# First four weight tiles turned on TensorE, first two tiles' matmuls by gradient quarters, column tables made behind the first rows

## Chip, cores and metric

One core of one Trainium2 chip runs the kernel. The metric is the device time of one execution in microseconds (us). TensorE (PE), VectorE (DVE), ScalarE (ACT) and GpSimd (POOL) compute; SyncE (SP) issues almost all DMAs. Each engine works through its own instructions in the order in which the program wrote them.

## The reference, cut to what matters

The forward pass of two blocks and all its gradients are computed in one launch, in bfloat16, with S = 2048, D = 448, F = 1792.

```python
def _A_ref(x, w_r, w_i):                    # spectral block
    X = rfft2(x.astype(float32)); X = X * (w_r + 1j * w_i)
    return irfft2(X, s=(S, D)).astype(bfloat16)

def _B_ref(x, w1, b1, w2, b2):              # MLP along the tokens
    h = _layernorm(x)
    u = gelu(einsum("bsd,sf->bdf", h, w1) + b1)
    return transpose(einsum("bdf,fs->bds", u, w2) + b2)

h  = x + _A_ref(_layernorm(x), A_w_r, A_w_i)
h2 = h + _B_ref(_layernorm(h), B_w1, B_b1, B_w2, B_b2)
# outputs: h2 and, from grad_out, the gradients of x, w_r, w_i, w1, b1, w2, b2
```

The part that the change touches first is one product of the backward pass, dg = w2 · grad_out (1792 x 2048 times 2048 x 448). It needs no result of the forward pass, only two inputs, so the kernel uses its matmuls as filling.

## The kernel before

**Stages.** First the forward Fourier transform: for each of 16 row groups, `row_a` (four 128-wide matmuls against a 128 x 128 table that is scaled by the layer norm, `scale_R`) and, three rows later, `row_b` (four 226-wide matmuls against the column tables `csF`). Each result is copied out of PSUM by `evac`, which picks ACT or DVE by a running estimate of their loads. After two rows of `row_b` a DMA on SP (line 668) reshapes the result into `D2`. Then `s2_stage` (line 671): four sets of small matmuls, the multiplication by the spectral weights on DVE (`w_mult`), small matmuls back, and 16 DMAs on SP (line 697) that reshape into `D3`. Then `inv_rows` (line 722), which needs all of `D3`, gives h. Then the MLP forward, backward and the spectral block backward. PE is nearly always busy behind `inv_rows`.

**The filling.** `dg_gen` (line 791) yields once per matmul of dg: 14 tiles of 128 rows of w2, each 16 matmuls of 448 columns that accumulate in one PSUM bank. `fill(n)` takes n of them at a place in the program. By the start of `s2_stage` 117 are taken, in the stage 95, the other 12 behind it. All 224 must be done before `inv_rows` is written.

**Its weights.** The matmul needs w2's tile with the tokens on the partitions, so `load_w2T` (line 301) loads it with a transposing DMA (line 306) on SP, into a ring of five buffers. Three are issued at the start, two in the row loop (`t in (1, 3)`), and then one whenever a tile is finished. Above `CAP` = 8 a finished tile's load is held back until the row loop is over (lines 907 to 909).

**Orders that matter.** SP's queue at the start is x rows 0 and 1, tile 0, x rows 2 and 3, four quarters of grad_out (`load_go`) among the rest of x, tiles 1 and 2, then the biases and the spectral weights (18 DMAs, line 573, spread over the row loop by `W_AT`). DVE and ACT make the 128-table (`gen_R`) and the column tables (`gen_fwd_d`: two chains on DVE, then two Sine activations on ACT) before the first layer norm statistics (`ln_stats`: line 82 is the helper that records every DVE and ACT instruction). ACT loads another function table when it goes from Sine to Sqrt and back; that is done at line 820 and at the first Sine of `gen_UV`. PE begins with 26 matmuls on zeros (line 360).

**Biases.** `load_biases` returns `turn`, called in `s2_stage` (line 914): two transposing DMAs on SP (line 786) and two copies on POOL that wait for them.

**PSUM.** `ps_mm()` gives one of four banks in turn, `ps_ff()` one of four others. Line 218 is every matmul but the small ones (line 223) and the transposes of `gen_inv_d` (line 545).

Of the kernel before, what the change touches and what calls it, by code (L numbers as in the profile page):

```python
# [10 lines left out]
BF16 = mybir.dt.bfloat16  # L11
# [6 lines left out]
P = 128  # L18
# [16 lines left out]
RESH_LAG = 1.1  # L35
ML_F = 4
SIDE = 2
CAP = 8
N_FILL_F = (6, 3, 20, 3, 24, 2)
N_FILL_B = (16, 16, 30, 8, 24, 8)  # L40
INV_SD = 1.0 / float(S * D)
# [81 lines left out]
def kernel(  # L123
# [54 lines left out]
    def ps_mm():  # L178
        return psum.tile([P, 512], F32, tag="mm", bufs=4, name="ps_mm")


    def evac(out, in_, scale=None):
        n = int(np.prod(in_.shape[1:]))
        if load[0] + sc.cost('copy', n, False) <= load[1] + ve.cost('tensor_copy', n, in_.dtype == BF16):
            if scale is None:
                sc.copy(out=out, in_=in_)
            else:
                sc.activation(out=out, in_=in_, func=ACT.Copy, scale=scale)
        elif scale is None:
            ve.tensor_copy(out=out, in_=in_)  # L190
        else:
            ve.tensor_scalar(out=out, in0=in_, scalar1=scale, scalar2=None, op0=ALU.mult)
# [24 lines left out]
    def mm(out, lhsT, rhs, start, stop):  # L217
        nc.tensor.matmul(out, lhsT=lhsT, rhs=rhs, start=start, stop=stop)  # L218
        clock[0] += int(np.prod(rhs.shape[1:])) / 2400.0
        run_due()  # L220
# [80 lines left out]
    def load_w2T():  # L301
        j = w2T_ring.i
        if j == NFB:
            return
        wT = w2T_ring.next()
        nc.sync.dma_start_transpose(out=wT, in_=B_w2[j * P:(j + 1) * P, :].rearrange("f (t c) -> f t c", c=P))  # L306
        w2Ts.append(wT)

    go_tp_d = grad_out[0].rearrange("(t p) d -> p t d", p=P)
    w2Ts = []  # L310

    def load_x(q):
        nc.sync.dma_start(out=xn[:, 4 * q:4 * q + 4, :], in_=x_pt[:, 4 * q:4 * q + 4, :])  # L313

    def load_go(q):
        nc.sync.dma_start(out=go_tp[:, 4 * q:4 * q + 4, :], in_=go_tp_d[:, 4 * q:4 * q + 4, :])  # L316
# [2 lines left out]
    load_w2T()  # L319
    nc.sync.dma_start(out=xn[:, 2:4, :], in_=x_pt[:, 2:4, :])  # L320
    load_go(0)
    load_go(1)
    load_x(1)
    load_go(2)
    load_go(3)
    load_x(2)
    load_x(3)
    load_w2T()
    load_w2T()
    gtail = rst[0:16, 2 * P:3 * P]  # L330
    gp_.memset(gtail, 0.0)
    nc.sync.dma_start(out=gtail[:, 0:64], in_=grad_out[0][S - 16:S, 3 * P:D])
# [24 lines left out]
    sc.activation(out=warm, in_=warm, func=ACT.Sin)  # L357
    nc.vector.memset(rAT[:, 0:512], 0.0)
    idle = ps_mm()
    for _ in range(26):  # L360
        nc.tensor.matmul(idle[:, 0:D], lhsT=rAT[:, 0:P], rhs=rAT[:, 0:D], start=True, stop=True)

    pcol = col()
# [55 lines left out]
    def gen_fwd_d():  # L419
        t = ftmp(576, 2, KW)  # L420
        t2 = ftmp(1028, 2, KW)
        q = ftmp(1536, 2, KW)
        q2 = ftmp(2048, 2, KW)
        js = []
        for o in (1.0, 225.0):
            js.append(col())
            ve.tensor_scalar(out=js[-1], in0=pcol, scalar1=2.0 / 896.0, scalar2=o / 896.0, op0=ALU.mult, op1=ALU.add)
        chains = []
        for w, u, v, ph in ((1, t, q, 0.0), (0, t2, q2, 0.25)):
            chain = []  # L430
            v_, s_ = Later(ve, chain), Later(sc, chain)
            for b in range(2):
                v_.tensor_scalar(out=u[:, b, :], in0=krow[:, 0:KW], scalar1=js[b], scalar2=ph, op0=ALU.mult, op1=ALU.add)
            v_.tensor_scalar(out=v, in0=u, scalar1=MAGIC, scalar2=MAGIC, op0=ALU.add, op1=ALU.subtract)
            v_.tensor_tensor(out=v, in0=u, in1=v, op=ALU.subtract)
            s_.activation(out=csF[:, w, :, :], in_=v, func=ACT.Sin, scale=s1)
            chains.append(chain)
        return [fn for pair in zip(*chains) for fn in pair]
# [159 lines left out]
    def scale_R(t):  # L598
        v = Rs_ring.next()
        ve.tensor_scalar(out=v, in0=Rm[:], scalar1=rstd_x[:, t:t + 1], scalar2=None, op0=ALU.mult)  # L600
        return v
# [33 lines left out]
    def row_a(t, R):  # L635
        pa = ps_ff()
        ft = folds[t // 2]
        for k in range(4):
            o = DC * (4 * (t % 2) + k)
            mm(pa[:, k * P:(k + 1) * P], lhsT=ft[:, o:o + P], rhs=R, start=True, stop=True)  # L640
        if t % 4 == 0:
            blks[t // 4] = blk_ring.next()
        evac(out=blks[t // 4][:, :, t % 4, :], in_=pa[:].rearrange("p (n x) -> p n x", x=8))
# [114 lines left out]
    def fill(n):  # L758
        while n > 0 and pending:
            try:  # L760
                next(pending[0])
                n -= 1
                if row_ops:
                    row_ops.pop(0)()
            except StopIteration:
                pending.pop(0)

    def drain():
        while pending:
            fill(1)  # L770
# [8 lines left out]
    def load_biases():  # L779
        gp_.memset(smr, 0.0)  # L780
        nc.sync.dma_start(out=smr[0:NFB, 0, :], in_=B_b1.rearrange("(j p) -> j p", p=P))
        nc.sync.dma_start(out=smr[:, 1, :], in_=B_b2.rearrange("(j p) -> j p", p=P))

        def turn():
            for i, dst in ((0, b1col), (1, b2col)):
                nc.sync.dma_start_transpose(out=smc[:, i, :], in_=smr[:, i, :])
                gp_.tensor_copy(out=dst[:], in_=smc[:, i, :])
        return turn


    def dg_gen():
        for j in range(NFB):
            wT = w2Ts.pop(0)
            pg = ps_mm()
            for t in range(NT):
                mm(pg[:, 0:D], lhsT=wT[:, t, :], rhs=go_tp[:, t, :], start=(t == 0), stop=(t == NT - 1))
                if t == NT - 1:
                    evac(out=dgu[:, j, :], in_=pg[:, 0:D])
                    if w2T_ring.i >= cap[0]:
                        held_w2.append(load_w2T)  # L800
                    else:
                        load_w2T()
                yield

    cap, held_w2 = [CAP], []
    pending.append(dg_gen())
# [4 lines left out]
    zero_pads()  # L811
    r_ops = []
    gen_R(Later(ve, r_ops), Later(sc, r_ops))
    fwd_ops = gen_fwd_d()
    for fn in r_ops:
        fn()
    for fn in fwd_ops:
        fn()
    nc.vector.memset(csF[:, 0, :, 0:1], 0.0)
    sc.activation(out=warm, in_=eps_x, func=ACT.Sqrt)  # L820
    base = ftmp(3072, 16, 16, 2)
    fix = ftmp(3584, 16)
# [9 lines left out]
        ln_stats(xn, t, mvx)  # L832
    sc.activation(out=rstd_x[:, 0:2], in_=mvx[:, 0:2, 1], func=ACT.Sqrt, bias=eps_x, scale=1.0)
    fold_prep(xn, 0)
    ve.tensor_scalar(out=ident[:], in0=krow[:, 0:P], scalar1=pcol, scalar2=None, op0=ALU.is_equal)
    ve.reciprocal(out=rstd_x[:, 0:2], in_=rstd_x[:, 0:2])
    Rs = {t: scale_R(t) for t in range(2)}
    for t in range(2, 4):
        ln_stats(xn, t, mvx)
    sc.activation(out=rstd_x[:, 2:4], in_=mvx[:, 2:4, 1], func=ACT.Sqrt, bias=eps_x, scale=1.0)  # L840
# [5 lines left out]
    gen_inv_cols(0)  # L846
    gen_inv_cols(1)
    fill(4)
    row_a(0, Rs.pop(0))
    for t in (4, 5):  # L850
        ln_stats(xn, t, mvx)
    for fn in rstd_of(4, 6):
        fn()
    fill(0)
    turn_biases = load_biases()
    Meter.side, Meter.every, Meter.count = [], 1, 0
    GROUPS = {0: (6, 8), 1: (8, 10), 3: (10, 12), 5: (12, 14), 7: (14, 16)}
    STATS = {0: (6, 7), 1: (8, 9), **{t: (t + 8,) for t in range(2, 8)}}
# [2 lines left out]
    for c in range(2):  # L861
        for e in range(2):
            sc.copy(out=Rp.rearrange("p (e a q b c) -> p c e a q b", e=2, c=2, q=8, a=2)[:, c, e],
                    in_=Rm[:, 64 * c + 32 * e:64 * c + 32 * e + 32].rearrange("p (q a b) -> p a q b", q=8, a=2))
    FILL_A = (4, 4, 4, 3, 3, 3, 3, 3, 3, 3, 3, 3, 3, 3, 3, 3)
    FILL_B = (0, 0, 0, 2, 2, 2, 2, 2, 2, 2, 2, 2, 2, 2, 2, 2)
    for t in range(NT):
        if t in (1, 3):
            load_w2T()
        if t + 1 < NT:  # L870
            row_a(t + 1, Rs.pop(t + 1))
        fill(FILL_A[t])
        if 1 <= t and t + 3 < NT:
            if t + 3 in (4, 8, 12):
                while Meter.side:
                    Meter.side.pop(0)()
            Rs[t + 3] = scale_R(t + 3)
        row_b(t - 3)
        if t == NT - 1:
            for i in range(t - 2, NT):  # L880
                row_b(i)
        if t % 2 and t < 12:
            fold_prep(xn, t // 2 + 2)
        for i in STATS.get(t, ()):
            ln_stats(xn, i, mvx)
        for _ in range(3 if t > 0 else 0):
            if next(uv, None):
                break
        if t in GROUPS:
            a, b = GROUPS[t]  # L890
            newton_gp(mvx[:, a:b, 1], rstd_x[:, a:b], slice(a, b))
        for _ in range(W_AT.get(t, 0)):
            next(w_loads, None)
        if t in INV_S:
            gen_inv_s(INV_S[t])
        if t == 2:
            gen_RT()
        fill(FILL_B[t])
# [8 lines left out]
    cap[0] = NFB  # L907
    while held_w2:
        held_w2.pop(0)()
    fill(30)  # L910

    def fwd_mult(s, j, x, y):
        if (s, j) == (2, 0):
            turn_biases()
        w_mult(x, set_of(W, s)[:, 2 * j:2 * j + 2], y, False)

    s2_stage(lambda s: set_of(Xs, s), fwd_mult, 9, 10, 0)
# [55 lines left out]
        nc.sync.dma_start(out=w2cs[i], in_=B_w2.rearrange("(j p) s -> p j s", p=P)[:, :, 256 * i:256 * i + 256])  # L973

    for i in range(3):
        load_w2c(i)
    inv_rows(h_consumer, N_FILL_F[5], Ring(aT_ring.views + [cut(rO, 1024, 4, P)]), (3, 7, 11, 15))
    norm_h(10)
# [2 lines left out]
    rstd_of_h(3)  # L981
    for t in range(12, NT):
        norm_h(t, t == 14)
    drain()
    nc.sync.dma_start(out=h_d.rearrange("(p t) d -> p t d", t=NT), in_=hn)

# [401 lines left out]
```

## Time and profile before

| | us |
|---|---|
| median of 3 runs | 355.53 (355.19 to 358.33) |
| the profiled execution, whole | 355.19 |
| its span in the profile | 353.4 |
| busy: PE, DVE, ACT, POOL | 333.7, 251.2, 196.9, 63.2 |

Rows of the timeline give start, duration, engine, line, operation, destination and source with their buffers, how many were merged, and in brackets how long the engine had been idle and what ended it. PE's matmul durations overlap, so its pace is read from start to start. "SPq" rows are SP's issues: the time is how long SP was taken by the instruction, not how long the transfer took. In the views by window each engine has busy time and number of instructions; then come the granted clock of PE (1.00 is full), the mean busy share of the 16 DMA engines (it can pass 1) and GB/s.

### The profile page before, as it was taken

The numbers are of one execution on the slowest core, as the hardware profiler recorded it, in microseconds if no ns is written. First come the engines' busy times: TensorE is split into PE (matmuls) and PEld (weight loads), VectorE is DVE, ScalarE is ACT, GpSimd is POOL, SyncE is SP. The second block draws the span as 40 slices with busy tenths as digits, with TensorE's granted clock in tenths as the row PEclk, the third lists the DMA queues.
The fourth block names the chain that finished last, engine by engine and source line by source line (L and its number), as shares of the span: only waits on it lengthen the run. The fifth ranks groups of instructions, "written<-read, shape, count | busy, mean of one in ns | idle before, by whom it ended". The sixth has DMA issues, their size and how long they took to land.

```text
span 353.4 us, 7799 instructions
## 1 busy us (share of the span) xinstructions
PE 333.7 (94%) x2819; PEld 174.1 (49%) x2819; DVE 251.2 (71%) x667; ACT 196.9 (56%) x430; POOL 63.2 (18%) x219
## 2 busy tenths in 40 slices
PE   8579989984999999999999999999999999999995
PEld 3346645442654555555555555554334434455552
DVE  8996426860594788858323888877489886589994
ACT  5458534543796653532331345557568877588872
POOL 5776000010132000001000211110000000055760
PEclk9989999998799999999999999999999999999999
DMA  8999999937985999679686789765889798998985
GB/s 213 302 180 180 180 255 196 195 109 211 314 229 225 299 355 249 168 189 297 168 192 159 170 186 184 182 99 167 234 237 243 242 252 238 282 248 262 228 309 203
DMA packets 147247, 78.03 MB, mean 221 GB/s; under 512 B 95688, under 2 KB 139976, under 8 KB 147080
## 3 DMA queue, kind: packets, MB, share of 16 engines
q1 hardware_dynamic: 146920, 77.13, 86.1%
q8 instruction: 22, 0.36, 0.4%
q10 hardware_dynamic: 288, 0.39, 0.3%
q14 instruction: 17, 0.14, 0.1%
HBM read 25.71 MB, written 22.04 MB: 135 GB/s over the span
## 4 chain that ended last, share of the span: by engine, by line
PE 82%; DMA 6%; DVE 4%; SPq 3%; ACT 2%; issue 1%; POOL 0%; DVEq 0%; ACTq 0%
PE ps_mm L218 66%; PE ps_ff L218 13%; DMA rE<-in_B_w_dram 3%; PE ps_ff L223 3%; DVE rS L82 2%; DMA r<-r 2%; DMA rO<-in_B_w_dram 1%; DVE r L82 1%; SPq L306 1%; SPq L573 1%; SPq L316 1%; SPq L668 1%; ACT rX L82 1%; SPq L313 0%; DVE rA L82 0%
## 5 line engine op out<-in xcount | busy, mean ns | idle before, releaser
L218 PEld LDWEIGHTS <-r 128*128 128x128 bf16 (+2 forms) x600 | 56.6, 107 | 50.7 <-issue 9.1
L218 PEld LDWEIGHTS <-rS 128*128 128x128 bf16 (+2 forms) x496 | 40.7, 98 | 36.6 <-issue 7.3
L82 ACT CAST rO<-ps_mm 128x512 bf16<-128x512 f32 (+1 forms) x70 | 37.3, 583 | 15.9 <-PE ps_mm L218 14.5
L218 PE MATMUL ps_mm<-rD,r 128*128 128x448 bf16 x224 | 44.5, 352 | 0.0
L218 PEld LDWEIGHTS <-rst 128*128 128x128 bf16 (+1 forms) x320 | 23.5, 97 | 31.3 <-issue 14.1
L218 PE MATMUL ps_mm<-rC,rE 128*128 128x448 bf16 x144 | 32.5, 360 | 4.1 <-DMA rE<-in_B_w_dram 2.3
L218 PE MATMUL ps_mm<-rB,r 128*128 128x448 bf16 x160 | 31.2, 352 | 0.1
L82 ACT CAST r<-ps_ff 128x452 bf16<-128x452 f32 x41 | 22.7, 587 | 11.5 <-PE ps_ff L223 6.2
L218 PE MATMUL ps_mm<-rG,rst 128*128 128x512 bf16 (+1 forms) x128 | 28.5, 380 | 0.3 <-ACT rO L82 0.3
L218 PE MATMUL ps_mm<-r,rst 128*128 128x512 bf16 (+2 forms) x144 | 27.4, 345 | 0.0
L82 ACT ACTIVATE r<-ps_mm,rstd_h 128x448 bf16<-128x448 f32 x16 | 10.1, 633 | 26.8 <-PE ps_mm L218 26.8
L82 DVE SCALAR_TENSOR_TENSOR r<-ps_mm,b2col,r 128x448 bf16<-128x448 f32 x16 | 10.9, 682 | 19.9 <-PE ps_mm L218 17.0
L82 ACT ACTIVATE r<-rC 128x448 bf16<-128x448 bf16 x16 | 9.1, 572 | 26.7 <-DMA out_dram<-r 20.5
L82 ACT ACTIVATE rG<-rG 128x896 bf16<-128x896 bf16 x14 | 13.3, 950 | 15.0 <-DVE rG L82 14.7
L218 PE MATMUL ps_mm<-rE,rS 128*128 128x448 bf16 x112 | 21.5, 352 | 0.0
L218 PEld LDWEIGHTS <-rO 128*128 128x128 bf16 (+1 forms) x165 | 15.1, 98 | 12.9 <-DMA rO<-in_B_w_dram 0.9
L82 ACT CAST rS<-ps_ff 128x512 bf16<-128x512 f32 x31 | 17.9, 580 | 5.7 <-PE ps_ff L218 5.3
L218 PEld LDWEIGHTS <-rE 128*128 128x128 bf16 x144 | 13.5, 99 | 14.2 <-DMA rE<-in_B_w_dram 2.5
L218 PE MATMUL ps_ff<-csI,rAT 113*128 113x224 bf16 (+1 forms) x108 | 20.3, 313 | 0.0
L1136 POOL TENSOR_SCALAR lcol<-lcol 128x1 f32<-128x1 f32 x16 | 8.5, 529 | 64.7 <-ACT r L82 64.7
L82 ACT CAST rAT<-ps_ff 113x512 bf16<-113x512 f32 x24 | 13.8, 584 | 10.6 <-PE ps_ff L218 10.3
L82 DVE SCALAR_TENSOR_TENSOR rA<-ps_ff,rA 128x448 bf16<-128x448 f32 x16 | 9.9, 619 | 12.0 <-PE ps_ff L218 11.9
(189 smaller groups left out, 602.6 us busy)
## 6 DMA issues: line engine op xcount, KB each, us to landing
out_dram<-rO SPq DMA_DIRECT2D x34, 256.0 KB
r<-in_B_w_dram SPq DMA_DIRECT2D x5, 1024.0 KB
r<-r SPq DMA_DIRECT2D x32, 113.0 KB
rS<-in_B_w_dram SPq DMA_DIRECT2D x4, 896.0 KB
r<-r SPq DMA_DIRECT2D x12, 226.0 KB
out_dram<-rG SPq DMA_DIRECT2D x10, 256.0 KB
rO<-in_B_w_dram SPq DMA_DIRECT2D x2, 1024.0 KB
rC<-in_grad_out_dram SPq DMA_DIRECT2D x4, 448.0 KB
```

What stands on the lines that cost most here:

```text
L82: fn(**kw)
L218: nc.tensor.matmul(out, lhsT=lhsT, rhs=rhs, start=start, stop=stop)
L223: nc.tensor.matmul(out, lhsT=lhsT, rhs=rhs, start=start, stop=stop)
L306: nc.sync.dma_start_transpose(out=wT, in_=B_w2[j * P:(j + 1) * P, :].rearrange("f (t c) -> f t c", c=P))
L316: nc.sync.dma_start(out=go_tp[:, 4 * q:4 * q + 4, :], in_=go_tp_d[:, 4 * q:4 * q + 4, :])
L573: nc.sync.dma_start(out=d_ap if store else sb, in_=sb if store else d_ap)
L668: defer(RESH_LAG, lambda: resh[0].dma_start(out=D2[u:u + 125:4, 8 * e:8 * e + 8].rearrange("p g c k -> p (g c k)"), in_=cs.rearrange("p x ...
L1136: gp_.tensor_scalar(out=m1, in0=ms, scalar1=-1.0 / D, scalar2=None, op0=ALU.mult)
```

## The change

Weight tiles 0 to 3 are loaded by plain DMAs into `rB` as they lie in memory. `turn_w2` transposes a tile by 16 PE transposes into two PSUM banks and copies each bank to the old place with one ACT copy of 1024 columns. Tile 0 is turned ahead of the first `row_a`, tile 1 behind the first four matmuls of dg, tiles 2 and 3 later. The first two tiles' matmuls are taken by quarters of grad_out: four of tile 0, four of tile 1, and so on. `gen_fwd_d` moves behind the first `row_a`, the identity matrix ahead. The plan of fills has the same sum up to `s2_stage` (117), with more in the rows t = 2, 3, 4 and 16 fewer behind the loop. `CAP` is 9, the idle matmuls are 20. The biases' transposing DMAs move to the weight loads behind `s2_stage`, and their copies to DVE behind `inv_rows`.

```diff
-CAP = 8
+CAP = 9
+N_NAT = 4
...
         wT = w2T_ring.next()
+        w2Ts[j] = wT
+        if j < N_NAT:
+            nc.sync.dma_start(out=w2n[:, j, :, :], in_=B_w2[j * P:(j + 1) * P, :].rearrange("f (t c) -> f t c", c=P))
+            return
         nc.sync.dma_start_transpose(out=wT, in_=B_w2[j * P:(j + 1) * P, :].rearrange("f (t c) -> f t c", c=P))
-        w2Ts.append(wT)
+
+    def turn_w2(j):
+        for h in range(0, NT, 8):
+            pt = ps_mm()[:].bitcast(BF16).rearrange("p (t c) -> p t c", c=P)
+            for t in range(8):
+                nc.tensor.transpose(pt[:, t, :], w2n[:, j, h + t, :], ident[:])
+            sc.copy(out=w2Ts[j][:, h:h + 8, :], in_=pt)
...
+    w2n = cut(rB, 0, N_NAT, NT, P)
...
     load_w2T()
     nc.sync.dma_start(out=xn[:, 2:4, :], in_=x_pt[:, 2:4, :])
     load_go(0)
+    load_w2T()
+    load_x(1)
     load_go(1)
-    load_x(1)
     load_go(2)
     load_go(3)
+    load_w2T()
     load_x(2)
+    load_w2T()
     load_x(3)
-    load_w2T()
-    load_w2T()
...
-    for _ in range(26):
+    for _ in range(20):
...
     def dg_gen():
-        for j in range(NFB):
-            wT = w2Ts.pop(0)
-            pg = ps_mm()
-            for t in range(NT):
...
+        pgs = {}
+        turns = {(0, 3): 1, (1, 15): 2, (2, 8): 3}
+        order = [(j, 4 * q + i) for q in range(4) for j in range(2) for i in range(4)]
+        for j, t in order + [(j, t) for j in range(2, NFB) for t in range(NT)]:
+            if not t:
+                pgs[j] = ps_mm()
+            mm(pgs[j][:, 0:D], lhsT=w2Ts[j][:, t, :], rhs=go_tp[:, t, :], start=(t == 0), stop=(t == NT - 1))
+            if (j, t) in turns:
+                turn_w2(turns[j, t])
...
-    fwd_ops = gen_fwd_d()
     for fn in r_ops:
         fn()
-    for fn in fwd_ops:
-        fn()
-    nc.vector.memset(csF[:, 0, :, 0:1], 0.0)
+    ve.tensor_scalar(out=ident[:], in0=krow[:, 0:P], scalar1=pcol, scalar2=None, op0=ALU.is_equal)
     sc.activation(out=warm, in_=eps_x, func=ACT.Sqrt)
...
-    ve.tensor_scalar(out=ident[:], in0=krow[:, 0:P], scalar1=pcol, scalar2=None, op0=ALU.is_equal)
     ve.reciprocal(out=rstd_x[:, 0:2], in_=rstd_x[:, 0:2])
     Rs = {t: scale_R(t) for t in range(2)}
+    turn_w2(0)
+    row_a(0, Rs.pop(0))
...
     fill(4)
-    row_a(0, Rs.pop(0))
+    fwd_ops = gen_fwd_d()
+    for fn in fwd_ops:
+        fn()
+    nc.vector.memset(csF[:, 0, :, 0:1], 0.0)
...
-    FILL_A = (4, 4, 4, 3, 3, 3, 3, 3, 3, 3, 3, 3, 3, 3, 3, 3)
+    FILL_A = (4, 4, 8, 12, 6, 3, 3, 3, 3, 3, 3, 3, 3, 3, 3, 3)
...
-        if t in (1, 3):
+        if t == 0:
             load_w2T()
...
-    fill(30)
+    fill(14)
...
-        if (s, j) == (2, 0):
-            turn_biases()
...
     for i in range(3):
+        if i == 2:
+            turn_biases()
         load_w2c(i)
...
+    place_biases()
     drain()
```

More of the change, by code (lines that the diff above doesn't have):

```diff
@@ L305, in load_w2T @@
         wT = w2T_ring.next()
+        w2Ts[j] = wT
+        if j < N_NAT:
+            nc.sync.dma_start(out=w2n[:, j, :, :], in_=B_w2[j * P:(j + 1) * P, :].rearrange("f (t c) -> f t c", c=P))
+            return
         nc.sync.dma_start_transpose(out=wT, in_=B_w2[j * P:(j + 1) * P, :].rearrange("f (t c) -> f t c", c=P))
-        w2Ts.append(wT)
+    def turn_w2(j):
[4 more added lines that the diff above has]
+            sc.copy(out=w2Ts[j][:, h:h + 8, :], in_=pt)
     go_tp_d = grad_out[0].rearrange("(t p) d -> p t d", p=P)
-    w2Ts = []
+    w2Ts = {}
+    w2n = cut(rB, 0, N_NAT, NT, P)
     def load_x(q):
@@ L786, in turn, with place @@
                 nc.sync.dma_start_transpose(out=smc[:, i, :], in_=smr[:, i, :])
-                gp_.tensor_copy(out=dst[:], in_=smc[:, i, :])
-        return turn
+        def place():
+            for i, dst in ((0, b1col), (1, b2col)):
+                ve.tensor_copy(out=dst[:], in_=smc[:, i, :])
+        return turn, place
     def dg_gen():
-        for j in range(NFB):
-            wT = w2Ts.pop(0)
-            pg = ps_mm()
-            for t in range(NT):
[L796 to L803, printed above, removed]
+        pgs = {}
[7 more added lines that the diff above has]
+                turn_w2(turns[j, t])
+            if t == NT - 1:
+                evac(out=dgu[:, j, :], in_=pgs.pop(j)[:, 0:D])
+                if w2T_ring.i >= cap[0]:
+                    held_w2.append(load_w2T)
+                else:
+                    load_w2T()
+            yield
     cap, held_w2 = [CAP], []
@@ L854 @@
     fill(0)
-    turn_biases = load_biases()
+    turn_biases, place_biases = load_biases()
     Meter.side, Meter.every, Meter.count = [], 1, 0
```

## The prediction

> **What bounds the kernel now.** The page's busy shares come first: PE is busy for 333.7 of 353.4 us, so time comes only from PE's holes or from work put on it. The view by windows says where the holes are.
>
> ```profile
> core 0: us, PE busy (x) PEld busy (x) DVE busy (x) ACT busy (x) POOL busy (x), PEclk, DMA share, GB/s
> 10.00:20.00 10.00, 4.27 (x31) 2.19 (x29) 9.06 (x38) 4.08 (x12) 7.57 (x34) 1.00 1.17 270
> 20.00:24.00 4.00, 4.00 (x21) 2.46 (x20) 3.85 (x14) 2.69 (x4) 2.86 (x14) 0.57 0.62 144
> 50.00:60.00 10.00, 8.40 (x131) 4.32 (x130) 4.82 (x10) 3.34 (x8) 0.00 (x0) 1.00 1.00 225
> 80.00:90.00 10.00, 5.04 (x29) 2.94 (x28) 0.27 (x1) 3.72 (x7) 0.00 (x0) 0.76 0.85 227
> ```
>
> Three holes: 5.7 us in 10 to 20, 1.6 in 50 to 60, 5.0 in 80 to 90. After the first and the third the granted clock falls to about a half. In 10 to 20 DVE is busy 9.06 of 10: it has no room. PE's timeline names what ended each hole, and the chain of waits does so for the third:
>
> ```profile
> 10.74 0.92 PE L218 MATMUL ps_mm<-rC,rE 128*128 128x448 bf16 x4 [0.54 <-DMA rC<-in_grad_out_dram]
> 13.05 0.92 PE L218 MATMUL ps_mm<-rC,rE 128*128 128x448 bf16 x4 [1.17 <-DMA rC<-in_grad_out_dram]
> 16.83 0.64 PE L218 MATMUL ps_ff<-rX,rS 128*128 128x128 bf16 x4 [1.58 <-DVE rS L82]
> 19.76 0.74 PE L218 MATMUL ps_mm<-rC,rE 128*128 128x448 bf16 x3 [2.29 <-DMA rE<-in_B_w_dram]
> ...
> 53.04 0.62 PE L223 MATMUL ps_ff<-r,Vt 32*32 32x452 bf16 x16 [1.38 <-DMA r<-rX]
> ...
> 56.37 1.69 PE L218 MATMUL ps_mm<-rC,rO 128*128 128x448 bf16 x8 [0.22 <-DMA rO<-in_B_w_dram]
> ```
>
> ```profile
> 79.14 0.99 ACT r L82 x2
> ...
> 81.86 5.39 DMA r<-r
> 87.25 0.35 issue
> 87.59 4.55 PE ps_ff L218 x23
> ```
>
> The row at 16.83 is `row_a(4)`: it waits for DVE, not for a load. The wait at 87.59 is for the last reshape into `D3`. Why that is late is in SP's queue:
>
> ```profile
> 8.25 10.87 SPq L306 DMA_TRANSPOSE rE<-in_B_w_dram  x2
> ...
> 51.91 4.25 SPq L306 DMA_TRANSPOSE rO<-in_B_w_dram  x2
> 56.26 9.14 SPq L306 DMA_TRANSPOSE rE<-in_B_w_dram  x3
> 65.50 1.99 SPq L306 DMA_TRANSPOSE rO<-in_B_w_dram  x1
> 67.59 3.28 SPq L697 DMA_DIRECT2D r<-r  x4
> 70.93 2.41 SPq L786 DMA_TRANSPOSE smc<-rst  x2
> 73.45 9.01 SPq L697 DMA_DIRECT2D r<-r  x12
> ```
>
> A transposing DMA holds SP for about 2 to 5 us, a plain load for about 0.5. From 51.91 to 82.46 SP has no pause: six transposes, then the 16 reshapes with two bias transposes between. The reshapes run behind their data and bunch at the end.
>
> **The front, step by step.** The idle matmuls end at about 7.7 instead of 8.8 (the last ones go at 0.18 each, six fewer). Transposes: those of line 545 took 0.27 for four (44.19 to 44.46 start to start), so 16 take 1.1 and all 64 take 4.3 us of PE. Bounds: 3.5 by the pace of 128-wide matmuls (0.22 for four), 6.9 by the length of the record (0.43 for four).
>
> The Trainium skill, TensorE: Matmul & The Clock Gate, part 4 (PE-mode transpose), speaks against this: about 275 ns for one transpose in a kernel, and transposes do not hold the clock up as matmuls do. By it 64 would be an estimated 17.6 us and the total some 13 us worse; the row at 44.19, at granted clock 1.00, says 0.07 us.
>
> The copies: eight of 1024 columns, all on ACT. A cast of 512 took 0.58, two in a row 1.07 (at 11.45): I take 0.97 each, between 0.95 (the 896-wide ACT row) and 1.16 (twice 0.58). What is queued behind them decides. ACT's order is: copies of tile 0, `row_a(0)`'s evacuation, the Sqrt for rows 2 and 3, copies of tile 1, Sine table, column tables. Tile 0's first half is turned at 8.4, so its copies end at 10.4, the evacuation (0.5) at 10.9, the Sqrt (0.3) at 11.2. DVE's reciprocal, at 10.76 before, waits for that Sqrt, and behind it stand in DVE's order: two scalings (0.5, to 11.7), the column chains now moved here (1.07 + 0.69 + 1.16 and two small ones, 3.1 in all, to 14.8), the memset of `csF` that waits for the Sine on ACT (0.65 after the last subtraction as before, 5.60 to 6.25: to 15.4), and only then the statistics of rows 4 to 7, Newton and fold. That stretch took from 11.86 to 16.83 before, 5.0 us. So `row_a(4)` starts at about 20.6, not 16.83. It gains nothing that x comes earlier.
>
> Before that PE has 20 matmuls of dg, four `row_a`, RTm and two tiles to turn, done by 16.2 (the quarters lie ready). So the hole is moved and is 4.4 us long. From 20.6 on PE has 97 matmuls (0.189 each: 18.3), 12 `row_a` (0.22: 2.6), 16 `row_b` (0.39: 6.2), the small ones (1.7), two tiles to turn (2.2) and about 0.3 of waiting for a copy: 31.3. The same sum for before (101 matmuls from 19.76, 11 `row_a`, no turning) is 29.4 against 31.9 measured to 51.65, the rest being mostly the half clock in 20 to 24 (1.7); the new hole brings the same: 2.5. So the filling ends at 54.4 instead of 51.65. Here before still waited for the reshape, until 53.04. Now `row_b` ends 20 matmuls and two table steps earlier, at 50.1; evacuation 0.5, issue 0.6 and 1.2 to landing give 52.4, hidden by the filling. `s2_stage` starts at 54.4: **+1.4**.
>
> **The back.** Tile 8 is now loaded in the row loop (`CAP`): PE's wait at 56.37 (11 matmuls from 53.89 end at 55.97) goes: **-0.4**. Tile 9 is then next, issued near 51, needed near 61: no wait. SP has five transposes, to about 64 at 2.6 each, and no bias transposes. The reshapes then keep up with their evacuations. The last four are evacuated at 78.28 to 80.13 before, plus 1.0 now: 79.3 to 81.1. Their transfers are 115.7 kB each; in 76 to 83 the DMA moved about 150 GB/s, and its first bytes came about 1.5 us after the issue at 73.45. 79.3 + 1.5 + 4 x 0.77 + some 0.7 gives 84.6. PE's filling ends at 82.63 + 1.0 = 83.6. So `inv_rows` starts at about 84.7 instead of 87.59: of the hole of 5.0 some 1.1 is left: **-3.9** beside the +1.0 carried in. A hole of 1.1 should not cost the clock (the ones of 0.5 and 1.2 did not). Before, h rows came at 90.63 and 92.38 and then every 0.985: at full clock the first saves about 0.9, the second 0.8: **-1.7**.
>
> For the relief a rule speaks against it: the Trainium skill, Advanced Engine Details and Errata, X-Bar Transpose (TRN2), says that transposing DMAs are as fast as regular ones. If so, fewer of them would give the back nothing, and the total would be that of the first rival; SP's rows of 2 to 5 us against 0.5 show where they differ, on the issuing queue.
>
> Smaller edits. The bias transposes (2.4 us of SP) go ahead of the third w2 load; behind that SP waited until 107.6 for the store of h anyway, so nothing, 2.4 if that cover went. Their copies on DVE are two small ones (0.3 at most) behind the last norms, needed by ACT's first bias add at 111.99. POOL loses a wait of 29.1 us whose followers (`nmean_h`) are needed only at 91. One Sine table load (1.28) moves from 21.84 on ACT to the front; counted there. From `inv_rows` on, the loads are written in the same order behind the same work, and PE's holes are small: the shift should last to the end.
>
> **Sum.** +1.4 - 0.4 - 3.9 - 1.7 = -4.6. The profiled execution took 355.19 (span 353.4 and 1.8 around it), 0.3 under the median: 350.6.
>
> **Rivals.** (1) The back does not close: the last reshapes still land 5.4 us after their issue, since w1's loads follow on the same DMA engines (share 0.8 and more from 84), and the clock still falls. Then +1.4 - 0.4: 356.2. For it: those transfers use half the engines (share 0.5) however early they come. Against: 12 of them were queued together, now four. (2) The front closes as intended: `row_a(4)` no later than 16.83, so 3.8 more: 346.8. Against it: ACT and DVE keep their written order. (3) Slower: the copies out of PSUM cost more than two casts. Four stand ahead of `row_a(4)` and the first halves of tiles 2 and 3 are waited for by PE, so each extra us per copy costs 6: the gain is gone at 0.97 + 4.6/6 = 1.7 us, and at 2.3 (four casts) the time is 358.6, with the back not closed 364. For it: no copy of that width from PSUM in the trace. Against: the 112-wide bf16 ones from PSUM went at 0.27 each, like 128-wide fp32.
>
> **Chances.** A change of this kernel under 1% (3.6 us) can hardly be told from none. The forecast 0.45, its own range 348 to 354: 0.32 of it is over 1% faster, 0.13 within. Rival 1 0.25 (0.03 faster, as the back may half close, 0.22 within). Rival 2 0.11. Rival 3 0.19 (0.03 within, 0.16 slower). Faster 0.46, same 0.38, slower 0.16. The range from 346.5 to 357.5 takes in rivals 1 and 2 and the start of 3, and leaves out the rest of rival 3 and of rival 2's lower side.
>
> **What would show it.** `row_a(4)` near 20.6 behind DVE, with the reciprocal of rows 2 and 3 waiting for ACT near 11.2; line 317's copies at about 1 us; the first of `s2_stage` near 54; no pause of the reshapes for bias transposes, `inv_rows` near 84.7 and the clock at 1.00 from 85 to 92. I am wrong if `row_a(4)` comes before 18, if the reshapes still end the last hole, or if the clock is down for long in the front.

## The result, and the profile after

| | before | after |
|---|---|---|
| median, us | 356.24 (352.67 to 359.25, 20 runs) | 353.03 (351.15 to 354.44, 20 runs) |
| profiled execution, us | 355.19 | 352.2 |
| its span, us | 353.4 | 350.4 |

The ratio is 0.9916 (95% interval 0.9893 to 0.9938). The kernel became 0.8% faster: under the 1% that the prediction called hard to tell from none. The medians differ by 3.2 us and the profiled executions by 3.0, about two thirds of the 4.6 us forecast. In the kernel after, the names of lines have moved: 82 is 83, 218 is 219, 223 is 224, 306 is 311, 668 is 681, 697 is 710, 786 is 799, 926 is 945; line 317 is the new transposes.

First the view by windows, in the same stretches as before.

```profile
core 0: us, PE busy (x) PEld busy (x) DVE busy (x) ACT busy (x) POOL busy (x), PEclk, DMA share, GB/s
10.00:20.00 10.00, 5.24 (x37) 2.82 (x35) 8.84 (x35) 6.25 (x14) 4.89 (x21) 0.88 1.14 322
20.00:24.00 4.00, 4.00 (x12) 1.58 (x11) 3.74 (x13) 0.90 (x2) 3.02 (x14) 0.50 1.17 189
50.00:60.00 10.00, 10.00 (x145) 5.29 (x144) 6.56 (x18) 5.02 (x15) 0.00 (x0) 1.00 1.07 206
80.00:90.00 10.00, 7.39 (x45) 4.17 (x43) 1.88 (x5) 4.57 (x10) 0.23 (x1) 0.83 0.89 234
```

The hole of 50 to 60 is gone, the one of 80 to 90 is halved (7.39 us busy instead of 5.04), and the front still has one of nearly 5 us, with the clock down for longer: 0.50 over all of 20 to 24, where it was 0.57 before. PE's timeline names the waits.

```profile
18.94 0.80 PE L219 MATMUL ps_ff<-rX,rS 128*128 128x128 bf16 x4 [4.20 <-DVE rS L83]
19.54 4.69 PE L219 MATMUL ps_mm<-rC,rE 128*128 128x448 bf16 x12
24.02 1.21 PE L317 MATMUL ps_mm<-ident,rB 128*128 128x128 bf16 x16
25.89 0.55 PE L219 MATMUL ps_mm<-rC,rE 128*128 128x448 bf16 x2 [0.27 <-ACT rE L83]
...
28.22 1.05 PE L317 MATMUL ps_mm<-ident,rB 128*128 128x128 bf16 x16
29.11 0.35 PE L219 MATMUL ps_mm<-rC,rE 128*128 128x448 bf16 x1
...
53.53 0.41 PE L224 MATMUL ps_ff<-r,Vt 32*32 32x452 bf16 x16
...
85.31 1.09 PE L219 MATMUL ps_ff<-RTm,r 128*113 128x128 bf16 x12 [2.61 <-issue]
```

The two waits of 0.54 and 1.17 for grad_out have gone, and `row_a(4)` (18.94) takes their hole: 4.20 us, ended by DVE. Twelve matmuls behind it take 4.5 us, twice the usual 0.189 each: that is the half clock. `s2_stage` starts at 53.53 (before 53.04) without waiting. The last row is `inv_rows`. Its bracket says "issue" and names nothing that ended the wait, and in the chain of waits nothing else stands there:

```profile
82.74 0.54 ACT rD L83
83.28 2.03 issue
85.31 9.87 PE ps_ff L219 x70
```

Before, "DMA r<-r" of 5.39 us stood in this place, and in runs 5 and 6 below the same wait is put down to it. So it is taken to be the last reshape here too, though its landing is not listed. SP's queue shows what became of the reshapes (the first of the five transposes, at 50.22, stands ahead of this view).

```profile
52.37 8.37 SPq L311 DMA_TRANSPOSE rE<-in_B_w_dram  x3
60.83 3.50 SPq L311 DMA_TRANSPOSE rO<-in_B_w_dram  x1
64.43 17.22 SPq L710 DMA_DIRECT2D r<-r  x16
81.75 3.64 SPq L945 DMA_DIRECT2D r<-in_B_w_dram  x2
85.49 4.16 SPq L945 DMA_DIRECT2D rO<-in_B_w_dram  x1
```

The 16 reshapes now take SP 17 us because they wait for their data, not the data for SP. The last four are evacuated by 80.20:

```profile
78.35 1.85 ACT L83 CAST r<-ps_ff 128x452 bf16<-128x452 f32 x4 [3.21 <-PE ps_ff L224]
```

They are the only ones under way then: from 78.5 to 80.0 the DMA engines moved nothing, and the first bytes of these four came at about 80.1.

In the front, ACT and DVE show the order that the prediction followed:

```profile
6.94 1.93 ACT L83 COPY rE<-ps_mm 128x1024 bf16<-128x1024 bf16 x2 [1.65 <-PE ps_mm L317]
8.75 0.60 ACT L83 CAST rS<-ps_ff 128x512 bf16<-128x512 f32 x1
9.22 0.32 ACT L83 ACTIVATE rstd_x<-mvx,cols 128x2 f32<-128x2 f32 x1
9.69 1.93 ACT L83 COPY rE<-ps_mm 128x1024 bf16<-128x1024 bf16 x2
```

```profile
9.57 0.17 DVE L83 RECIPROCAL rstd_x<-rstd_x 128x2 f32<-128x2 f32 x1 [1.27 <-ACT rstd_x L83]
...
12.01 1.16 DVE L83 TENSOR_TENSOR r<-r 128x452 f32<-128x452 f32 x2
14.02 0.62 DVE L83 BATCH_NORM_STATS2 stats<-rA 128x6 f32<-128x448 bf16 x1 [0.85 <-issue]
```

Copies of tile 0, evacuation, Sqrt, and DVE's reciprocal waits for it. Two copies take 1.81 us to the next start: 0.91 each.

By place, the change of the profiled execution is: the stage's start +0.49 us; tile 8's wait gone, so that the second set starts at 57.94 against 57.98 (-0.53, of which 0.39 is the stretch up to tile 8's matmuls and 0.14 the first set itself); the rest of the stage +0.11; the last hole 2.61 instead of 4.96 (-2.35), which brings `inv_rows` from 87.59 to 85.31; PE's long run behind `inv_rows` from 105.95 to 103.25 (-0.42 more, the clock); -0.30 over all the rest. Sum: -3.0, the difference of the spans.

### The profile page after: what moved, and what is told of

Its sections match the earlier page's. It is cut to its first block, busy times and chain, and to the rows that moved or that the text cites. A ratio compares the mean times of both kernels' runs of the same rounds, so it can differ in the third digit from the quotient of the medians.

```text
span 350.4 us, 7916 instructions
## 1 busy us (share of the span) xinstructions
PE 333.9 (95%) x2868; PEld 176.0 (50%) x2877; DVE 253.3 (72%) x671; ACT 202.7 (58%) x436; POOL 64.4 (18%) x217
## 4 chain that ended last, share of the span: by engine, by line
PE 88%; DVE 6%; ACT 2%; issue 2%; POOL 0%; DVEq 0%; ACTq 0%
PE ps_mm L219 70%; PE ps_ff L219 12%; PE ps_ff L224 3%; DVE rS L83 2%; DVE r L83 2%; PE ps_mm L374 1%; ACT rE L83 1%; PE ps_mm L317 1%; DVE stats L83 1%; ACT rX L83 0%; DVE rA L83 0%; ACT rD L83 0%; ACT rC L83 0%; DVE rO L83 0%; DVE rstd_x L83 0%
## 5 line engine op out<-in xcount | busy, mean ns | idle before, releaser
L219 PE MATMUL ps_mm<-rC,rE 128*128 128x448 bf16 x144 | 33.8, 372 | 1.1 <-ACT rE L83 1.1
L219 PE MATMUL ps_mm<-rG,rst 128*128 128x512 bf16 (+1 forms) x121 | 26.8, 380 | 1.1 <-issue 0.8
L83 ACT CAST r<-ps_ff 128x452 bf16<-128x452 f32 x39 | 21.6, 591 | 7.5 <-PE ps_ff L224 6.1
L83 DVE SCALAR_TENSOR_TENSOR r<-ps_mm,b2col,r 128x448 bf16<-128x448 f32 x16 | 10.9, 683 | 19.8 <-PE ps_mm L219 16.9
L219 PE MATMUL ps_mm<-rC,rO 128*128 128x448 bf16 x80 | 18.1, 353 | 0.0
```

The lines of the kernel that those rows point to most:

```text
L83: fn(**kw)
```

## The experiments

Ratios are to the kernel before in the same batch of runs. Three batches ran, not all on the same chip (before: 357.17, 356.43 and 355.18 us), so times from different batches are compared by their ratios. The changed kernel itself ran in none of the three: a comparison with its 0.9916 is one across batches. Each trace is one execution.

### 1 and 2: the biases, each way

The first puts the bias transposes and their POOL copies of the changed kernel back into the stage. The second moves only them, in the kernel before.

```diff
     def fwd_mult(s, j, x, y):
+        if (s, j) == (2, 0):
+            turn_biases()
...
-        if i == 2:
-            turn_biases()
```

> The changed kernel with the bias transposes and POOL copies put back into the stage. Theory (fewer weight transposes alone let SP keep up): in the changed kernel SP pauses twice between groups of reshapes, so 2.4 us more are covered; inv_rows starts within 0.5 us of 85.3 and the time is that of the changed kernel within 1 us. Rival (the bias transposes were what held the reshapes back): the last hole grows again, inv_rows near 87, time 1.5 to 3 us above the changed kernel.

> The kernel before with only the bias transposes moved behind the stage. Theory (any 2.4 us off SP there lets the reshapes catch up): the first four reshapes still begin near 67.6, the next ones directly behind them, the last four near 79; inv_rows near 85.5 instead of 87.6, time 2 to 3 us under before, so most of the whole change without its front. Rival (the six weight transposes are what counts): inv_rows at 87 or later, time within 1 us of before.

Measured: 352.56 (ratio 0.9886, 0.9837 to 0.9935) and 355.24 (0.9948, 0.9917 to 0.9979). With the biases back in the stage the changed kernel keeps all its gain (`inv_rows` at 85.60). In the kernel before, moving them is worth half a per cent alone: `inv_rows` at 86.73 instead of 87.59, although the stage began 0.95 later there, behind a wait of 1.60 for a D2 reshape ahead of which this edit touches nothing.

```profile
86.73 1.50 PE L218 MATMUL ps_ff<-RTm,r 128*113 128x128 bf16 x12 [2.66 <-issue]
```

So neither expectation of run 2 fits as a whole: from the last evacuation to `inv_rows` the time fell from 7.5 to 5.2 us, as the theory has it, but the late stage took back 0.95, and `inv_rows` came neither near 85.5 nor at 87.

### 3: the column tables later

The changed kernel with `gen_fwd_d` and the memset of `csF` moved into the row loop at t = 1, behind the fold of rows 4 and 5.

```diff
-    fwd_ops = gen_fwd_d()
-    for fn in fwd_ops:
-        fn()
-    nc.vector.memset(csF[:, 0, :, 0:1], 0.0)
...
             fold_prep(xn, t // 2 + 2)
+        if t == 1:
+            for fn in gen_fwd_d():
+                fn()
+            nc.vector.memset(csF[:, 0, :, 0:1], 0.0)
```

> The changed kernel with the column tables made behind the statistics, Newton and fold of rows 4 to 7 (in the row loop at t = 1) instead of ahead of them. Theory (the hole before row_a(4) is DVE's queue: 3.0 us of tables, their wait for ACT's Sine of 0.9): row_a(4) at 15 to 15.6 instead of 18.9, no half clock from 18 to 25, row_b(0) near 19, the stage 4 to 6 us earlier than 53.5, time 3.5 to 6 us under the changed kernel. Rival (the front is hidden by SP's queue of weights and reshapes, which is full from 20 to 50): the stage less than 2 us earlier, time within 1.5 us of the changed kernel.

Measured: 350.80 (0.9837, 0.9792 to 0.9882). By the ratios that is some 2.8 us under the changed kernel, between the theory's 3.5 to 6 and the rival's 1.5. PE's timeline:

```profile
15.70 0.65 PE L219 MATMUL ps_ff<-rX,rS 128*128 128x128 bf16 x4 [0.87 <-DVE rS L83]
...
19.95 0.56 PE L219 MATMUL ps_ff<-csF,rS 112*128 112x226 bf16 x4 [0.45 <-ACT rS L83]
21.96 0.74 PE L219 MATMUL ps_mm<-rC,rE 128*128 128x448 bf16 x2 [1.44 <-ACT rE L83]
23.20 2.45 PE L219 MATMUL ps_mm<-rC,rE 128*128 128x448 bf16 x6
```

`row_a(4)` comes 3.2 us earlier and its hole shrinks from 4.20 to 0.87: that hole was the place of the column tables in DVE's order. Of the 3.2 us about 2.0 are kept to the stage (a set of it at 64.30 instead of 66.39) and to `inv_rows` (83.39). The rest went into waits that came up behind: ACT now makes Sine tables and tile 2's copies late (0.45 and 1.44), and PE still meets a stretch at half clock (six matmuls in about 2.2 us from 23.20).

### 4: a fence ahead of w1's loads

The changed kernel with a small DMA on SP that reads `D3` and so holds w1's loads until all reshapes have landed.

```diff
+    fence_d = dram.tile([P, 8], BF16, name="fence_d")
+    flush()
+    nc.sync.dma_start(out=fence_d, in_=D3[:, 0, 0, 0:8])
     w1cs = [load_w1c(jp) for jp in range(3)]
```

> The changed kernel with one tiny extra DMA that reads all of D3's rows ahead of w1's loads on SP, so that these begin only when the last reshape has landed. Theory (w1's loads share the DMA engines with the last reshapes): the last one lands 1 us earlier or more, inv_rows near 84.0, the hole near 1.3, time 1 to 2 us under the changed kernel. Rival (the reshapes' own latency is what is left): inv_rows within 0.4 us of 85.3, time within 1 us or above.

Measured: 351.45 (0.9868, 0.9813 to 0.9924); against the changed kernel's 0.9916 the difference lies within the intervals. The place is clear in the trace: `inv_rows` came at 84.45, 4.42 us behind the last evacuation (80.03) instead of 5.11 (80.20 to 85.31).

```profile
84.34 0.38 SPq L951 DMA_DIRECT2D fence_d<-r  x1
84.45 0.85 PE L219 MATMUL ps_ff<-RTm,r 128*113 128x128 bf16 x12 [1.92 <-issue]
```

So 0.7 us of the remaining hole is sharing the DMA engines with w1's loads; the other 1.9 stays without them. Here the last four reshapes were alone: the DMA engines moved data from about 79.9 to 83.8 and then nothing until w1's loads, and PE began 0.7 us behind the last bytes.

### 5 and 6: what gives SP its room

The first of these takes the changed kernel back to `CAP = 8` and puts the biases back: turning and quarters stay, but six transposes and two bias transposes stand in the stage. The other is the kernel before with `CAP = 9` and nothing else.

```diff
-CAP = 9
+CAP = 8
```

> The changed kernel with CAP back at 8 and the bias transposes and their POOL copies back in the stage: tiles 0 to 3 are still loaded as they lie and turned on PE, but SP has six weight transposes and two bias transposes between 52 and 82 again. Theory (what the changed kernel gained is room in SP's queue during the stage, and turning alone gives nothing): the last reshapes are issued until about 82 to 83, inv_rows starts at 87 or later behind a hole of 4.5 to 5.5 us that a DMA ends, the clock is at half for two windows, and the time is that of the kernel before within 1 us (ratio 0.997 to 1.003). Rival (the earlier row loop and the quarters of dg give the gain): inv_rows stays near 85.3 and the time at a ratio near 0.990.

> The kernel before with CAP = 9 and nothing else: tile 8's transposing load goes into the row loop, five are left for the stage, the biases stay. Theory (turning buys the place in SP's queue that tile 8 needs: before, SP is full from 20 to 52): the transpose pushes the last D2 reshapes back, s2_stage starts at 54.5 to 56 behind a DMA wait instead of 53.0, and of the 2.5 to 3 us that inv_rows gains against the stage's start 1.5 to 3 are given back: ratio 0.995 to 1.000. Rival (the place was there all along, and turning on PE was not needed): s2_stage starts before 53.7, inv_rows near 85.5, ratio near 0.989 as with the changed kernel.

Measured: 352.93 (0.9933, 0.9902 to 0.9965) and 357.61 (1.0055, 1.0023 to 1.0086). The theory of the first fell: with as many transposes in the stage as before the gain is nearly whole (the interval overlaps the changed kernel's). The SP queue of its profiled execution (351.06, the fastest of its twelve) tells why.

```profile
42.82 6.68 SPq L681 DMA_DIRECT2D r<-rX  x4
49.59 4.20 SPq L311 DMA_TRANSPOSE rO<-in_B_w_dram  x2
53.88 9.57 SPq L311 DMA_TRANSPOSE rE<-in_B_w_dram  x3
63.55 1.90 SPq L311 DMA_TRANSPOSE rO<-in_B_w_dram  x1
65.56 3.29 SPq L710 DMA_DIRECT2D r<-r  x4
68.91 2.40 SPq L799 DMA_TRANSPOSE smc<-rst  x2
71.42 9.49 SPq L710 DMA_DIRECT2D r<-r  x12
```

```profile
84.48 0.85 PE L219 MATMUL ps_ff<-RTm,r 128*113 128x128 bf16 x12 [2.52 <-DMA r<-r]
```

It is the same queue as before, but it begins at 49.59 instead of 51.91. Before, SP issued without a pause up to that place; here it has three transposes instead of five between 20 and 45 and waits for the last D2 data (6.68 us for four reshapes that took 2.56). So it is free 2.3 us earlier, while the stage begins almost where it did (52.90). SP takes up the last 12 reshapes at 71.42 instead of 73.45, and that is enough. The second shows that the room was not there without turning, and dearer than expected:

```profile
56.31 0.82 PE L223 MATMUL ps_ff<-r,Vt 32*32 32x452 bf16 x16 [5.17 <-DMA r<-rX]
...
90.00 0.85 PE L218 MATMUL ps_ff<-RTm,r 128*113 128x128 bf16 x12 [2.71 <-DMA r<-r]
```

Tile 8's transpose in the full row loop pushed the D2 reshapes back; the hole closed behind the stage (4.96 to 2.71) and opened ahead of it (1.38 to 5.17), with the clock at half from 53.7 to 60.5.

Six of the kernels give a rule. Margin is from SP's taking up the last 12 reshapes to the end of ACT's last evacuation; latency is from there to `inv_rows`.

| kernel | margin, us | latency, us |
|---|---|---|
| before | 6.7 | 7.5 |
| 5: CAP 8, biases in the stage | 8.0 | 5.0 |
| 6: before with CAP 9 | 8.4 | 5.2 |
| 2: biases moved, else before | 8.6 | 5.2 |
| 1: biases in the stage | 9.8 | 4.9 |
| after | SP waits for the data | 5.1 |

Between 6.7 and 8.0 lies the point from which more room in SP's queue buys nothing: 2.4 us of latency, and no more, whichever edit makes the room. This is argued from the table; no run swept the margin itself. In runs 3 and 8 SP waits for the data as in the changed kernel, and their latency was 5.3 and 5.4.

### 7: tables late and fence together

Edits 3 and 4 in one kernel.

> The changed kernel with both edits that helped by themselves: the column tables generated in the row loop, and the small load that reads D3 ahead of w1's loads. Theory (they act at different places, front and last hole, and their gains add): row_a(4) near 15.7 as with late tables alone, inv_rows near 82.7 behind a hole near 2, ratio 0.980 to 0.983 against the kernel before. Rival (the stage is set by its own work and loads, so that only one of them counts): ratio 0.984 to 0.987.

Measured: 350.29 (0.9865, 0.9822 to 0.9908); `row_a(4)` at 16.24, `inv_rows` at 83.30 behind a hole of 1.90. The interval takes in the rival's numbers and part of the theory's. The ratio itself is the rival's and no lower than run 3's 0.9837, so the time gives no sign that the two gains add. The latency does repeat: 78.89 to 83.30, 4.41 us, as in run 4.

### 8: every copy twice

The changed kernel with each of ACT's eight 1024-wide copies issued twice.

```diff
             sc.copy(out=w2Ts[j][:, h:h + 8, :], in_=pt)
+            sc.copy(out=w2Ts[j][:, h:h + 8, :], in_=pt)
```

> The changed kernel with each of ACT's eight copies out of PSUM issued twice, so that a turned half tile costs ACT 1.8 us instead of 0.9. Theory (the copies lie on the path of row_a(4), and PE waits for those of tiles 2 and 3, as the prediction put it: 6 us per us and copy): row_a(4) goes from 18.94 to 21.5 to 22.7, the waits at tiles 2 and 3 grow to about 1 us each, and the time rises by 4 to 5.5 us, to that of the kernel before (ratio 0.998 to 1.005). Rival (DVE's own queue sets row_a(4) and the copies lie beside it): row_a(4) before 20, and the time rises by under 2 us.

Measured: 357.44 (1.0057, 1.0029 to 1.0086), 1.4% above the changed kernel's ratio, or 5.0 us. Here are ACT and DVE:

```profile
7.80 4.02 ACT L83 COPY rE<-ps_mm 128x1024 bf16<-128x1024 bf16 x4 [2.63 <-PE ps_mm L317]
11.72 0.30 ACT L83 ACTIVATE rstd_x<-mvx,cols 128x2 f32<-128x2 f32 x1
11.91 4.01 ACT L83 COPY rE<-ps_mm 128x1024 bf16<-128x1024 bf16 x4
15.94 1.28 ACT L83 ACT_TABLE_LOAD   x1
```

```profile
14.37 1.16 DVE L83 TENSOR_TENSOR r<-r 128x452 f32<-128x452 f32 x2
18.32 0.62 DVE L83 BATCH_NORM_STATS2 stats<-rA 128x6 f32<-128x448 bf16 x1 [2.79 <-issue]
18.35 0.06 DVE L871 MEMSET csF<- 128x2 bf16 x1
```

Tile 0's copies push the Sqrt and so the reciprocal; tile 1's push the Sine table, and DVE stands 2.79 us (0.85 before the edit) at the memset of `csF` until ACT's Sine is done. `row_a(4)` moved to 23.24, 4.3 us, more than expected, as four more copies lie ahead of it (4 x 0.91 = 3.6), and the first turn itself came 0.9 later in this execution. The price of 6 us per us and copy is about right: 5.0 for 0.91 is 5.5.

### 9 and 10: less filling ahead of the stage

The last hole is latency with 22 matmuls of dg under it. Nine of the 14 matmuls ahead of the stage are put there too: in run 9 on the changed kernel, in run 10 with edits 3 and 4 as well.

```diff
-    fill(14)
+    fill(5)
```

> The changed kernel with nine matmuls of dg less ahead of the stage (fill(5) where it has fill(14)); they are then run by the drain behind the stage. Theory (the last hole of 2.6 us is the latency from the last evacuation to the landing of the last reshape, about 4.6 us, with 22 matmuls of dg under it, while s2_stage starts about 1.7 us after its data could be there): the stage starts 1.5 to 1.7 us earlier without a DMA wait, the drain's 31 matmuls cover most of the latency, inv_rows starts near 83.7 behind a hole of 0.6 to 1.2 instead of 2.6, the clock after it stays at 1.00, and the time falls by 1.5 to 3 us against the changed kernel (ratio 0.983 to 0.987). Rival (the D2 reshapes land no earlier than the stage starts now): s2_stage waits for a DMA for about what was taken away, and the time stays within 0.5 us of the changed kernel.

> All three edits that are thought to help: the column tables in the row loop, the small load of D3 ahead of w1's loads, and nine matmuls of dg less ahead of the stage. Theory (the front's hole and the last hole are separate places, so the gains add): inv_rows near 81.7 behind a hole under 1, time 347 to 349, ratio 0.975 to 0.982. Rival (the stage then waits for its own D2 reshapes): a DMA wait of 1 us or more at the start of s2_stage and a time of 350 or more.

Measured: 351.15 (0.9905, 0.9871 to 0.9939) and 348.66 (0.9839, 0.9788 to 0.9891). In run 9 the hole shrank as expected, to 1.08, but `inv_rows` came at 84.74, not 83.7: in that execution `row_a(4)` was at 19.83, 0.9 later than in the changed kernel's, and the stage met a wait of 0.92 for `csI`, which no expectation had named. Its ratio lies outside the theory's 0.983 to 0.987, and by it run 9 can't be told from the changed kernel; the rival had said so, but for a DMA wait that did not come. In run 10 the time, `inv_rows` (81.48) and the hole came as the theory said, but the ratio lies above its 0.975 to 0.982. Its interval ends just below the changed kernel's (0.9891 against 0.9893), and in the batch that the two runs share, five of its six times lie below run 9's lowest of 349.64. It is no lower than run 3's 0.9837, so it is not shown that the fence and the smaller filling add to what the late tables give. Its profiled execution (347.11; the fastest of the six took 347.09) has:

```profile
50.71 0.37 PE L224 MATMUL ps_ff<-r,Vt 32*32 32x452 bf16 x4 [0.92 <-DVE csI L83]
...
81.48 0.85 PE L219 MATMUL ps_ff<-RTm,r 128*113 128x128 bf16 x12 [0.18 <-issue]
```

```profile
10.00:20.00 10.00, 8.46 (x71) 5.00 (x67) 8.94 (x35) 6.69 (x15) 5.94 (x25) 1.00 1.12 342
20.00:24.00 4.00, 2.28 (x17) 1.24 (x17) 3.75 (x14) 2.35 (x4) 2.52 (x10) 1.00 0.88 187
50.00:60.00 10.00, 9.29 (x170) 4.88 (x170) 7.15 (x18) 4.73 (x11) 0.00 (x0) 1.00 1.08 189
80.00:90.00 10.00, 9.59 (x78) 6.09 (x77) 5.90 (x17) 7.05 (x19) 1.40 (x7) 1.00 0.66 168
```

The last hole is gone (0.18), the front's is down to 1.5 us in 10 to 20 and 1.7 in 20 to 24 (the waits of run 3), and the granted clock is 1.00 in all four stretches, all in this one execution. By its ratio this version is 1.6% faster than before, and faster than the changed kernel by the edge of the intervals only.

## Why the prediction was right, and where it was not

The direction and the places were right, the sum was 1.6 us too good. The time lies within a range that was 11 us wide, in the part of it, the forecast's own but under 1%, that had a chance of 0.13. Two of the prediction's three signs of being wrong did show: the reshapes still end the last hole (its own sum had them end one of 1.1 us), and the clock was at half for 6.8 us in the front. Errors also cancelled: the front was 0.9 us better than forecast, largely by luck, while the last hole and the clock behind it were 2.8 worse. By its own steps:

- **The copies on ACT.** 0.97 us each was forecast, 0.91 measured. Run 8 shows that the price was worth asking for: at twice the copies the gain was gone and more. Rival 3 had the mechanism, but its condition was not met.
- **The transposes on PE.** 1.1 us for 16 was forecast; 0.89 was measured where the clock was at 1.00 (28.22 to 29.11, start to start) and 1.05 where the half clock ended in it (24.02 to 25.07): 0.056 to 0.066 us each. The 275 ns of the Trainium skill, TensorE: Matmul & The Clock Gate, part 4 (PE-mode transpose), is the duration of one transpose (the page sets another figure against it as "63% of dur"). Here the record of one is 0.22 us long (219 ns, the median of 64), but the next starts 0.056 to 0.066 behind it. So the prediction's 64 times 275 took a duration for a pace, and the measured pace decides. Whether transposes alone would hold the clock up is not shown: here they stand between matmuls.
- **The front, +1.4.** The mechanism was right to the instruction, the size was off: +0.5. From the reciprocal to `row_a(4)` 9.4 us were forecast (11.2 to 20.6) and 9.37 measured (9.57 to 18.94). Only the start was wrong: the idle matmuls ended at 6.3, not 7.7 (the first transpose starts at 6.29). They run at half pace at first, and this execution left that pace at 3.8 us, the one of before at 6.7. With the start of before, the 20 would have ended at 7.7 as forecast (15 of them 0.37 us apart, five 0.19), so this part of the gain is luck. In other executions of the same front `row_a(4)` came at 18.79 to 19.83 (runs 4, 1, 5 and 9). Of the 1.7 us won here 0.8 was lost again: from `row_a(4)` to the stage 33.8 were forecast and 34.6 taken, as the clock was at half from 17.5 to 24.3, two windows of 3.4 us, not one; in runs 5 and 9 it was one (19.1 to 22.5 and 19.8 to 23.2).
- **Tile 8, -0.4.** Right: 0.39 of the -0.53.
- **The last hole, -3.9.** This term failed most: -2.35. `inv_rows` was forecast for 84.7 and came at 85.31, but the filling ended 0.9 earlier than forecast (82.70), so 2.6 us of hole were left, not 1.1. The step that failed is "79.3 + 1.5 + 4 x 0.77 + some 0.7". It allowed 5.3 us from the first of the last four evacuations to the landing, and 6.6 were taken (78.35 to about 84.96, if the landing stands 0.35 us ahead of `inv_rows` as in before). About 0.7 of the 1.3 that was missing is w1's loads on the same DMA engines, which run 4 took away. The rest is in two terms of the sum that run 4 shows by themselves: the first bytes came 1.7 us behind the start of the first evacuation (78.18 to 79.9), not 1.5, and the four transfers took 3.9 us (to 83.8), not 4 x 0.77 = 3.1. Rival 1 had named that sharing, but took it for the whole latency.
- **What relieved the back.** The prediction put it down to five transposes instead of six and the biases gone from the stage. Either was more than enough, and run 5 shows that neither was needed, since the loads that need no transposing DMA had already ended SP's row loop 2.3 us earlier. The smaller edit, moving the biases, was costed at nothing, and costs nothing in the changed kernel (run 1); in the kernel before it is worth half a per cent (run 2). The X-Bar Transpose (TRN2) section of Advanced Engine Details and Errata in the Trainium skill, that transposing DMAs are as fast as regular ones, would have meant 356.2 by the prediction. No run here timed those transfers. What counts here is how long SP is held: 1.9 to 3.5 us for a transposing load in the row loop and the stage (6.2 for the first one), 0.6 for a reshape that does not wait, and one transpose too many in the row loop cost 3.8 us of hole at the stage (run 6).
- **The clock, -1.7.** A hole of 1.1 was to leave the clock alone; one of 2.6 was left, and the clock went to half once more, from 85.8 to 89.2, instead of for two windows (85.2 to 92.0). PE stood still in the first part of those two, so before had 4.5 us of work at half clock behind the start of `inv_rows`, and after 3.4. Gained: 0.4.

What is open is how much of the medians' 3.2 us is clock. Each timed run lists its mean granted clock. It was 0.982 on average over 52 timed runs of before and 0.988 over 20 of after; at 3.4 us a window, 0.005 is one window. Within one kernel, runs with 0.005 less clock took about 1.1 us longer (pooled over all kernels here; the correlation is 0.62 in size). By that some 1.5 us would go with the clock. The two profiled executions don't show it: 0.986 and 0.983, three windows each. No run held the clock fixed. Nor did a run leave out the quarters of grad_out or the turning alone, so what each gives is not separated.

## What to carry to other kernels

By the table of margins, a queue that issues transfers is relieved only up to the point where the transfers keep up with their data; beyond it more room buys nothing, so read the latency from the last producer to the consumer, and then look for work to put under that latency (nine matmuls moved from ahead of the stage to behind it cut the last hole to 1.08 us in run 9 and, with the two other edits, to 0.18 in run 10; no queue edit brought it under 1.90, though run 9's time did not show the gain). When an engine's steps are moved, write out the order of every engine that they wait for: here tables that moved behind an ACT wait took away what earlier loads had given. And a term that rests on the start of the clock, or on an execution's luck with it, needs its own range.

## What the runs showed of the hardware

- Half-clock stretches of 3.4 us, or twice that, follow holes of PE, but not each of them: holes of 1.90 to 2.90 us ahead of `inv_rows` were followed by one in after and in runs 1 to 4 and 6 to 8, and by none in run 5 (2.52); holes of 1.08 and 0.18 (runs 9 and 10) by none. Within an execution the changes of the clock lie whole steps of 3.41 us apart (17.5, 85.8 and 89.2 in after), and these steps fall differently in each. In after the hole of 2.61 lies in one step; in run 5, counted from its changes at 19.1 and 22.5, the hole is split into 2.0 and 0.5. Whether that decides is not shown.
- The first idle matmuls started 0.37 us apart, until 3.8 us in after and 6.7 in before, and the later ones 0.19, while the granted clock read 1.00 throughout: this pace at the start is not in that column.
- A single reshape of about 113 kB that was issued last took 3.8 us to land in runs 5 and 6, and 5.39 in before, where SP was later against its data.
